# Sums over the features of a linear-attention branch: from VectorE reductions to identity products on TensorE

## The chip, the core and the metric

The kernel runs on one core of a Trainium2 chip. The metric is device time in microseconds (us) for one execution of the whole program. Five engines work side by side, each with its own instruction queue: PE (TensorE, matrix products; PEld is its loading of weights), ACT (ScalarE), DVE (VectorE), POOL (GpSimd) and SP (SyncE, which here issues DMAs). They are tied together by semaphores only. Matrix products read SBUF and write PSUM; ACT and DVE carry results out of PSUM.

## The reference

The inputs are x (1 x 2048 x 512), two sets of projections, and a gate vector. The result is `g * a + (1 - g) * b` with `g = sigmoid(sum(x * gate_w))`. Both branches have 32 heads of 16 features.

- Branch B is plain softmax attention over 2048 keys, followed by an output projection.
- Branch A is linear attention. For queries and for keys it forms `p = q @ w_phi` (16 values per head) and takes `phi = concat(softmax(p), softmax(-p))`, 32 features per head. Then `kv = phi_k^T v`, `z = sum(phi_k)`, and the output is `(phi_q kv) / (phi_q z + 1e-6)`, again followed by an output projection.

The change concerns the denominators of those two softmaxes of branch A: for each token and each head the sum of 16 exponentials of `p` and of 16 exponentials of `-p`, so 64 sums per token, for keys and for queries.

## The kernel before

Branch B fills most of the time. The scores are made transposed, 128 keys by 512 queries at a time: 4 chunks of queries, 32 heads and 16 key tiles give 2048 such tiles, one matrix product each (`qk_mm`, L1283). They are cut into 32 blocks of 64 tiles. In each block a fixed number of tiles (the list `DN`, 712 in all) is exponentiated by DVE and POOL with integer arithmetic (`add_group`, L1360 or L1350 for two tiles at once, then `shifted`, L1336, on POOL), and the other 1336 go in pairs to ACT, 668 instructions of 128x1024 (`add_exp`, L1374). For ACT two pairs of PSUM banks are used in turn, so PE writes a pair of scores while ACT works on the other. The products with V accumulate in one more bank, psO (`pv_mm`, L1395). The last three PSUM banks (`MISC`) are shared by all else: the scores for DVE, every projection, and everything of branch A.

Branch A is spread through the run, one tile of 128 tokens (`st`) at a time. `phi(1, st)` projects the keys (four products, L1044), ACT takes both exponentials out of PSUM (two instructions, L1651), and DVE sums 16 neighbours for each head and sign (`tensor_reduce`, 128x1024 to 128x64, L1657). After each second tile DVE takes the reciprocals of both tiles' sums (L1671). The values of the same tokens are projected (`va_fill`) and written to SBUF twice, once multiplied by the reciprocal for each sign (L1633, two DVE instructions), and POOL copies the reciprocals beside them (L1637). `kv_half` then multiplies `phiK` with these scaled values over eight token tiles. `phi(0, st)` does the same for queries, but there only the ratio of the two sums is formed (reciprocal L1664, product L1666) and the second half of the features is multiplied by it (`scaled_q`, L1683); the tile goes to DRAM, comes back transposed by DMA (`q_turn`), and meets `kv` in `z_rest` (L1740, L1746) and `q_rest` (L1753, L1759). With 16 token tiles for keys and 16 for queries there are 32 sums on L1657, in 16 pairs.

`fill` adds a group of products on PE that takes a bank of `MISC`, cut into operations of `chunk` products; `drain` adds the instruction that reads the bank and, with `last`, frees it. `Plan.layout` orders all operations on the five queues by priorities and estimated durations. Where PE would have nothing to do it puts in an idle operation, four products with zero weights (`zero_mm`, L1385). `Plan.settle(MOVES)` then changes that order by hand-kept lists: for each engine pairs (from, to) of places in its queue, two-tile merges on DVE, banks, and under "drop" the places on PE of idle operations that are left out. So the order on each queue is fixed when the program is built. Before the change PE's queue has 2653 operations, 111 of them idle ones; "drop" names 173 places, and the highest place on PE to which an operation is moved is 2652, the last one.

Features in `phiK`, `EA` and the weights `Wp` lie in the order head group (8), sign (2), head in the group (4), feature (16), the feature innermost. `mask64` and `mask4` cut the products of unlike heads from `kv`.

Of the kernel before, what the change touches and what calls it, by code (L numbers as in the profile page):

```python
# [11 lines left out]
ALU = mybir.AluOpType  # L12
AX = mybir.AxisListType

S = 2048
D = 512
# [49 lines left out]
VA_LAG = 2  # L66
# [25 lines left out]
    ),  # L92
    "act": (
# [3 lines left out]
    ),  # L97
# [786 lines left out]
def _build(ctx, nc, A_x, A_wqkv, A_w_phi, A_wo, B_wqkv, B_wo, gate_w, out):  # L884
# [20 lines left out]
    Ty = sb([128, 2, 2048], name="Ty")  # L905
    vaug = sb([128, NT, VAW], name="vaug")
    vAf = sb([128, 8 * 8 * 2 * 68], name="vA")
    vA = vAf[:].rearrange("p (a b s c) -> p a b s c", a=8, b=8, s=2)
    phiK = sb([128, 8, 1024], name="phiK")
    Ebuf = sb([128, EPAIRS, 512 * (SZ[0] + SZ[1])], name="E")  # L910

# [728 lines left out]
    def phi(qk, st, prio):  # L1640
# [18 lines left out]
        if b == 0:  # L1659
            return  # L1660
# [257 lines left out]
```

## Time and profile before

| what | value |
|---|---|
| median of 3 runs | 680.75 us (680.67 to 681.05) |
| the profiled execution | 680.21 us, its span 678.2 us |
| PE busy | 669.4 us (99%) |
| ACT busy | 654.9 us (97%) |
| DVE busy | 618.0 us (91%) |
| POOL busy | 383.4 us (57%) |
| ACT on the 668 exponentials of branch B (L1374) | 624.7 us |
| DVE on the 32 sums (L1657) | 38.7 us |
| granted TensorE clock | 1.000 |

The span runs from the first to the last instruction. A group of instructions is named by its line, engine and operation, then what it writes and reads ("psS<-qz_t,kTB_t" is a product of two tiles into PSUM). After the bar stand the busy time of the group and the mean of one in nanoseconds. PE's rows overlap: a matrix product's row lasts until its modelled end, while the next one starts earlier, so the distance between starts tells PE's pace and the length of a row doesn't. A busy PE includes the idle operations.

### The profile page before, as it was taken

To read this page: it belongs to the slowest core of one execution; us is meant where nothing else is said; L and a number is where in the kernel's file an instruction comes from. 1 tells how busy PE (TensorE), PEld (TensorE's weight loads), DVE (VectorE), ACT (ScalarE), POOL (GpSimd) and SP (SyncE) were. 2 spreads that over 40 slices of the span, in tenths; PEclk is the share of its full clock that TensorE was granted. 3 is DMA by queue.
4 is the path that set the end of the run, shared out by engine and by line. 5 is a ranking of instruction groups with operands and counts; after the bars stand their busy time and mean duration, and the time that the engine had idled before them with its cause. 6 is when DMAs were issued, how large, how long until landed. Compare 5 with 4: busy or idle time off the path is not lost.

```text
span 678.2 us, 20089 instructions
## 1 busy us (share of the span) xinstructions
PE 669.4 (99%) x8563; PEld 217.5 (32%) x8563; DVE 618.0 (91%) x959; ACT 654.9 (97%) x739; POOL 383.4 (57%) x419
## 2 busy tenths in 40 slices
PE   8999999999999999999999999999999999999997
PEld 4333333333332333323322223322333233333333
DVE  4699899899999999988999989999899999999983
ACT  6999999999999999999998999999999999999995
POOL 7066367453656545455477665676464755565843
PEclk9999999999999999999999999999999999999999
DMA  6810101001010000100113022121321224123221
GB/s 132 159 32 11 31 14 27 11 10 23 7 27 11 10 20 10 28 7 15 22 37 89 26 68 73 46 51 47 69 85 26 70 74 105 34 65 75 65 71 41
DMA packets 67465, 30.90 MB, mean 46 GB/s; under 512 B 52697, under 2 KB 62297, under 8 KB 67377
## 3 DMA queue, kind: packets, MB, share of 16 engines
q1 hardware_dynamic: 66368, 28.95, 17.8%
q8 instruction: 67, 1.10, 0.7%
q10 hardware_dynamic: 576, 0.52, 0.2%
q0 software_dynamic: 432, 0.15, 0.2%
q14 instruction: 22, 0.17, 0.1%
HBM read 7.87 MB, written 8.88 MB: 25 GB/s over the span
## 4 chain that ended last, share of the span: by engine, by line
PE 78%; ACT 14%; DVE 5%; DMA 1%; issue 0%; SPq 0%; DVEq 0%
PE psS L1283 28%; PE psO L1395 27%; PE psS L1044 14%; ACT E_t L1374 13%; PE psO L1385 3%; DVE Tx_t L1360 2%; PE psS L1148 1%; PE psS L1135 1%; PE psS L1696 1%; DMA Lq_t<-ld 1%; DVE Ty_t L1360 1%; ACT EA_t L1651 1%; DMA ld<-Tf_t 1%; PE psS L1753 1%; PE psS L996 0%
## 5 line engine op out<-in xcount | busy, mean ns | idle before, releaser
L1374 ACT ACTIVATE E_t<-psS 128x1024 bf16<-128x1024 f32 x668 | 624.7, 1061 | 11.9 <-PE psS L1283 11.4
L1283 PE MATMUL psS<-qz_t,kTB_t 32*128 32x512 bf16 x2048 | 285.3, 384 | 3.1 <-ACT E_t L1374 1.1
L1360 DVE TENSOR_SCALAR Tx_t<-psS 128x512 int16<-128x512 f32 x232 | 154.5, 684 | 10.4 <-PE psS L1283 8.9
L1283 PEld LDWEIGHTS psS<-qz_t,kTB_t 32*128 32x128 bf16 x2048 | 74.0, 91 | 245.4 <-ACT E_t L1374 108.9
L1395 PE MATMUL psO<-E_t,vaug_t 128*32 128x512 bf16 (+1 forms) x1336 | 109.7, 384 | 0.0
L1336 POOL INT64_ADD vA_t<-vA_t x69 | 67.8, 988 | 25.7 <-PE psO L1395 21.6
L1360 DVE TENSOR_SCALAR Ty_t<-psS 128x512 int16<-128x512 f32 x106 | 71.0, 681 | 4.3 <-PE psS L1283 3.3
L1336 POOL INT64_ADD Ty_t<-Tx_t x28 | 28.2, 1007 | 51.5 <-DVE Tx_t L1360 41.6
L1336 POOL INT64_ADD Ty_t<-Ty_t x39 | 39.6, 1016 | 19.5 <-PE psO L1395 18.4
L1395 PE MATMUL psO<-vA_t,vaug_t 128*32 128x512 bf16 (+1 forms) x494 | 47.3, 382 | 0.0
L1360 DVE TENSOR_SCALAR oT_t<-psS 128x512 int16<-128x512 f32 x60 | 40.1, 683 | 4.1 <-PE psS L1283 3.5
L1395 PE MATMUL psO<-Ty_t,vaug_t 128*32 128x512 bf16 (+1 forms) x414 | 42.0, 384 | 0.0
L1044 PE MATMUL psS<-Wp_t,xT_t 128*32 128x512 bf16 x512 | 40.4, 382 | 0.1
L1360 DVE TENSOR_SCALAR Tz_t<-psS 128x512 int16<-128x512 f32 x58 | 38.1, 684 | 2.4 <-PE psS L1283 2.1
L1044 PE MATMUL psS<-xT_t,WB_t 128*32 128x512 bf16 x464 | 40.0, 383 | 0.0
L1385 PE MATMUL psO<-xT_t,zero_t 128*32 128x512 bf16 x408 | 38.8, 385 | 0.5 <-DVE Tf_t L1489 0.4
L1395 PEld LDWEIGHTS psO<-E_t,vaug_t 128*32 128x32 bf16 x1336 | 26.4, 95 | 39.6 <-issue 30.4
L1360 DVE TENSOR_SCALAR vA_t<-psS 128x512 int16<-128x512 f32 x52 | 34.9, 683 | 1.3 <-PE psS L1283 1.1
L1360 DVE TENSOR_SCALAR WAT_t<-psS 128x512 int16<-128x512 f32 x50 | 33.4, 682 | 2.2 <-PE psS L1283 1.9
L1360 DVE TENSOR_SCALAR Wp_t<-psS 128x512 int16<-128x512 f32 x46 | 30.8, 679 | 0.4 <-PE psS L1283 0.3
L1336 POOL INT64_ADD WoB_t<-oT_t x17 | 17.2, 1013 | 19.4 <-DVE oT_t L1360 15.8
L1395 PE MATMUL psO<-Tx_t,vaug_t 128*32 128x512 bf16 x268 | 27.8, 387 | 0.0
(162 smaller groups left out, 904.5 us busy)
## 6 DMA issues: line engine op xcount, KB each, us to landing
dpq<-EA_t SPq DMA_DIRECT2D x16, 256.0 KB, 2.3
Rb_t<-lr SPq DMA_DIRECT2D x120, 32.0 KB, 1.8
dpo<-kv_t SPq DMA_DIRECT2D x16, 128.0 KB, 1.7
qz_t<-qz_t SPq DMA_DIRECT2D x120, 16.0 KB, 1.8
Tf_t<-Tf_t SPq DMA_DIRECT2D x60, 32.0 KB, 2.0
WB_t<-in_B_wqkv_dram SPq DMA_DIRECT2D x3, 384.0 KB, 4.3
out_dram<-WvA_t SPq DMA_DIRECT2D x8, 128.0 KB, 2.0
out_dram<-WB_t SPq DMA_DIRECT2D x6, 128.0 KB, 1.9
```

The lines of the kernel that those rows point to most:

```text
L1044: ins = e.matmul(out[32 * i:32 * i + 32, :], lhsT=lhsT[:, 32 * i:32 * i + 32], rhs=rhs, start=start, stop=stop, tile_position=(0, 32 * i))
L1135: mms = [lambda e, ap, i=i, t=t: e.matmul(ap[:, 128 * i:128 * (i + 1)], lhsT=xT[:, t, NQ * c + 128 * i:NQ * c + 128 * (i + 1)], rhs=W_B[:, ...
L1148: mms = [lambda e, ap, i=i, t=t: e.matmul(ap[:, 256 * i:256 * (i + 1)], lhsT=xT[:, t, NQ * c + 128 * (2 * hf + i):NQ * c + 128 * (2 * hf + ...
L1283: return e.matmul(bank, lhsT=kT_B[32 * i:32 * i + 32, ROW[b // 2] % 2, 128 * kt:128 * (kt + 1)], rhs=qz[32 * i:32 * i + 32, b // 2 % 4, b ...
L1336: op = P.add("pool", P64 + W64 * size, d_prio(g["ts"][0]) - 5.0 + (0.0 if key == "s" else M_LATE), lambda e: e.int64_add(words(dst), words ...
L1360: ops.append(drain(f, mm, "dve", 0.70, d_prio(d), lambda e, ap, q=q: e.tensor_scalar(quarter(tb, q).bitcast(I16), ap, EXPB, 0.0, op0=ALU.a ...
L1374: op = P.add("act", EXP_OVH + 0.4267 * n, 0.0, lambda e: e.activation(Ebuf[:, j // 2 % EPAIRS, 512 * SZ[0] * (j % 2):512 * SZ[0] * (j % 2) ...
L1385: ins = e.matmul((psO if bank is None else bank)[32 * i:32 * i + 32, :], lhsT=zero[:], rhs=xT[:, 0, 0:NQ], start=bank is not None, stop=ba ...
L1395: return e.matmul(psO[32 * i:32 * i + w, :], lhsT=vaug[:, kt, o:o + w], rhs=rhs, start=start, stop=stop, tile_position=(0, 32 * i), skip_g ...
L1651: ins = e.activation(dst.rearrange("p (g s c) -> p s g c", s=2, c=64)[:, sgn, :, :], ap.rearrange("p (g c) -> p g c", c=64), ACTF.Exp, sca ...
L1696: ins = e.matmul(ap[64 * s:64 * s + 64, 68 * gg:68 * gg + 68], lhsT=phiK[:, m, 128 * g + 64 * s:128 * g + 64 * s + 64], rhs=vA[:, m, g, s, ...
L1753: mms = [lambda e, ap, g=g: e.matmul(ap[:, 64 * g:64 * g + 64], lhsT=qT(g)[:, 128 * j:128 * (j + 1)], rhs=kzbd[:, g, 0:64], start=True, st ...
```

## The change

The sums over 16 features leave DVE. For each pair of token tiles PE now multiplies an identity matrix with the exponentials, once for each of the 16 features, and accumulates: 32 products of 128x128 weights with 64 columns, in four operations of eight, into 128 columns of one `MISC` bank (`fill` named S). DVE takes the reciprocals directly out of that bank (keys: one instruction for both tiles; queries: the reciprocal of the second half, and a copy of the first half to `statq` for the later denominator). The projection of the values now waits for these products (`after = [mm]`) and not for a DVE operation.

So that one product reads four neighbouring elements at a time, the features are laid out with the four heads of a group innermost: head group, sign, feature, head. That is done where `Wp` is copied from PSUM (a permuted output), and `scaled_q`, the masks and the views of `stat` and `statq` follow. `mask4` is made by a DVE sum of the identity and one POOL copy in place of a POOL fill and four POOL copies. The two multiplications of V become one DVE instruction with 128x1024 outputs, and `vA` has the sign ahead of the head group.

All lists of `MOVES` are other ones. "drop" names 207 places (173 before), the highest place on PE is 2696 (2652 before). `DN`, the slots of ACT and all other constants stay. Of `MOVES` only ACT's list is shown; its first numbers are places in the queue as laid out, its second ones the places to which operations are moved.

```diff
@@ -63,7 +63,7 @@
-VA_LAG = 2
+S_PRIO = -2.0
@@ -80,341 +80,350 @@
 MOVES = {
...
     "act": (
-        (87, 80), (105, 85), (127, 104), (133, 122), (131, 124), (136, 128), (149, 145), (151, 148), (158, 167), (179, 220), (181, 222), (185, 241),
-        (197, 244), (211, 249), (215, 257), (238, 263), (244, 279), (268, 287), (277, 356), (304, 375), (331, 378), (379, 412), (383, 419), (413,
-        456), (415, 459), (442, 505), (444, 509), (484, 525), (486, 553), (516, 584), (520, 589), (564, 619), (568, 630),
+        (87, 79), (105, 82), (127, 101), (132, 114), (137, 123), (139, 126), (155, 141), (157, 146), (177, 166), (198, 218), (200, 221), (201, 241),
+        (218, 244), (238, 251), (242, 256), (244, 266), (249, 281), (268, 288), (277, 357), (330, 376), (332, 379), (350, 412), (359, 419), (390,
+        454), (394, 458), (408, 504), (417, 509), (427, 524), (446, 552), (480, 584), (488, 589), (530, 618), (543, 630),
...
@@ -905,7 +914,7 @@
     vAf = sb([128, 8 * 8 * 2 * 68], name="vA")
-    vA = vAf[:].rearrange("p (a b s c) -> p a b s c", a=8, b=8, s=2)
+    vA = vAf[:].rearrange("p (a s b c) -> p a s b c", a=8, b=8, s=2)
@@ -1030,10 +1039,8 @@
     wbd_ops = [dma("pool", -4, lambda e, j=j: e.dma_start(Wbd[16 * j:16 * j + 16, :, 16 * j:16 * j + 16], wphi_v[j]),
                    [("Wbd", j)], reads=["Wbd0"], name=f"wbd{j}", issue=0.8, lat=3.0) for j in range(8)]
     P.join_writes(wbd_ops, "Wbd")
-    pool(0.1, -2, lambda e: e.memset(mask4[:], 0.0), writes=["mask40"], name="mk0")
-    P.join_writes([P.add("pool", 0.15, -2, lambda e, q=q: e.tensor_copy(mask4[32 * q:32 * q + 32, 2 * (q % 2):2 * (q % 2) + 2],
-                                                                      half2[32 * q:32 * q + 32, :]), reads=["half2", "mask40"],
-                         name=f"mk1{q}") for q in range(4)], "mask4")
+    small(lambda e: e.tensor_reduce(quad[:, 0:4], ident[:].rearrange("p (k j) -> p j k", j=4), AX.X, ALU.add), ["ident"], ["quad"], "mk0", -2)
+    pool(0.15, -2, lambda e: e.tensor_copy(mask4[:], quad[:, 0:4]), reads=["quad"], writes=["mask4"], name="mk1")
     pool(0.2, -2, lambda e: e.tensor_copy(mask64[:].rearrange("p (j c) -> p j c", c=16), mask4[:].unsqueeze(2).to_broadcast([128, 4, 16])),
          reads=["mask4"], writes=["mask64"], name="mk2")
@@ -1618,7 +1625,8 @@
                                            rhs=Wbd[:, r, :], start=True, stop=True) for r in range(KT)]
         f, mm = fill(prio, mms, ["Wbd"] + [("WAT", 4 * qk + r) for r in range(KT)], name=f"W{qk}{t}", chunk=4,
                      dur=0.07, cols=128)
-        wp_ops.append(drain(f, mm, "dve", 0.69, prio, lambda e, ap: e.tensor_copy(Wp[:, t, D * qk:D * (qk + 1)], ap),
+        wp_ops.append(drain(f, mm, "dve", 0.69, prio, lambda e, ap: e.tensor_copy(
+            Wp[:, t, D * qk:D * (qk + 1)].rearrange("p (a f j) -> p a j f", j=4, f=DH), ap.rearrange("p (a j f) -> p a j f", j=4, f=DH)),
                             writes=[("Wp", qk, t)], name=f"We{qk}{t}"))
     va_ops = []
@@ -1628,13 +1636,13 @@
         f, mm = fill(prio, proj([xT[:, t, 128 * st:128 * (st + 1)] for t in range(KT)],
                                 [WvA[:, t, :] for t in range(KT)]), ["WvA"] + xk(st // 4), name=f"VA{st}", after=after, kind="col")
         va_ops.append(mm)
-        by = stat[:, b, :].rearrange("p (g s j) -> p g s j", s=2, j=4)
-        for s in range(2):
-            drain(f, mm, "dve", 0.70, prio, lambda e, ap, s=s: e.tensor_tensor(
-                vA[:, m, :, s, 0:64].rearrange("p g (j d) -> p g j d", j=4), ap.rearrange("p (g j d) -> p g j d", g=8, j=4),
-                by[:, :, s, :].unsqueeze(3).to_broadcast([128, 8, 4, DH]), ALU.mult),
-                reads=[("rs", b), ("ss", b)], writes=[("vA", m, s)], name=f"VAe{st}.{s}", last=s == 1)
-        P.add("pool", 0.3, prio, lambda e: e.tensor_copy(vA[:, m, :, :, 64:68], by), reads=[("rs", b), ("ss", b)],
+        by = stat[:, b, :].rearrange("p (s g j) -> p s g j", s=2, j=4)
+        drain(f, mm, "dve", 1.24, prio, lambda e, ap: e.tensor_tensor(
+            vA[:, m, :, :, 0:64].rearrange("p s g (j d) -> p s g j d", j=4),
+            ap.rearrange("p (g j d) -> p g j d", g=8, j=4).unsqueeze(1).to_broadcast([128, 2, 8, 4, DH]),
+            by.unsqueeze(4).to_broadcast([128, 2, 8, 4, DH]), ALU.mult),
+            reads=[("rs", b)], writes=[("vA", m, s) for s in range(2)], name=f"VAe{st}")
+        P.add("pool", 0.3, prio, lambda e: e.tensor_copy(vA[:, m, :, :, 64:68], by), reads=[("rs", b)],
               writes=[("vA", m, 2)], name=f"VAr{st}")
     def phi(qk, st, prio):
@@ -1652,25 +1660,27 @@
                                    ap.rearrange("p (g c) -> p g c", c=64), ACTF.Exp, scale=1.0 - 2.0 * sgn)
             return ins
         drain(f, mm, "act", 0.98, -4, both, writes=[dkey], name=f"ex{qk}.{st}")
-        e3 = dst.rearrange("p (g f) -> p g f", f=DH)
-        sums, skey = (stat[:, b, :], ("ss", b)) if qk else (statq[:, st % 8, :], ("sq", st % 8))
-        P.add("dve", 1.22, prio, lambda e: e.tensor_reduce(sums, e3, AX.X, ALU.add), reads=[dkey], writes=[skey],
-              name=f"ss{qk}.{st}")
         if b == 0:
             return
+        es = [(phiK[:, i % 8, :], ("phiK", i % 8)) if qk else (EA[:, i % 2, :], ("EA", i % 2)) for i in (st - 1, st)]
+        mms = [lambda e, ap, n=n, f=f: e.matmul(ap[:, 64 * n:64 * n + 64].rearrange("p (s g j) -> p s g j", s=2, j=4), lhsT=ident[:],
+                                                rhs=es[n][0].rearrange("p (g s f j) -> p f s g j", s=2, f=DH, j=4)[:, f],
+                                                start=(f == 0), stop=(f == DH - 1)) for n in range(2) for f in range(DH)]
+        f, mm = fill(S_PRIO + prio, mms, [k for _, k in es] + ["ident"], name=f"S{qk}.{st}", chunk=8, dur=0.042, cols=64)
         if qk == 0:
-            both_q = statq[:, st % 8 - 1:st % 8 + 1, :].rearrange("p b (g s j) -> p (b g) s j", s=2, j=4)
-            r3 = ratio[:].rearrange("p b (g j) -> p (b g) j", j=4)
-            P.add("dve", 0.4, prio, lambda e: e.reciprocal(r3, both_q[:, :, 1, :]), reads=[("sq", st % 8 - 1), ("sq", st % 8)],
-                  writes=["ratio"], name=f"rs{qk}.{st}")
-            P.add("dve", 0.25, prio, lambda e: e.tensor_tensor(r3, r3, both_q[:, :, 0, :], ALU.mult),
+            three = lambda ap: ap[:, 0:128].rearrange("p (b s c) -> p b s c", b=2, s=2)
+            drain(f, mm, "dve", 0.55, prio, lambda e, ap: e.reciprocal(ratio[:], three(ap)[:, :, 1, :]), writes=["ratio"],
+                  name=f"rs{qk}.{st}", last=False)
+            drain(f, mm, "dve", 0.25, prio, lambda e, ap: e.tensor_copy(statq[:, st % 8 - 1:st % 8 + 1, 0:32], three(ap)[:, :, 0, :]),
+                  writes=[("sq", st % 8 - 1), ("sq", st % 8)], name=f"rp{qk}.{st}")
+            P.add("dve", 0.25, prio, lambda e: e.tensor_tensor(ratio[:], ratio[:], statq[:, st % 8 - 1:st % 8 + 1, 0:32], ALU.mult),
                   reads=["ratio", ("sq", st % 8 - 1), ("sq", st % 8)], writes=["ratio"], name=f"rt{qk}.{st}").lock = True
             for i in (st - 1, st):
                 scaled_q(i, prio)
             return
-        P.add("dve", 0.62, prio, lambda e: e.reciprocal(stat[:], stat[:]), reads=[("ss", 0), ("ss", 1)],
+        drain(f, mm, "dve", 0.96, prio, lambda e, ap: e.reciprocal(stat[:], ap[:, 0:128].rearrange("p (b c) -> p b c", b=2)),
               writes=[("rs", 0), ("rs", 1)], name=f"rs{qk}.{st}")
-        after = [P.ops[-VA_LAG]]
+        after = [mm]
         for i in (st - 1, st):
             va_fill(i, prio, after)
@@ -1678,8 +1688,8 @@
     def scaled_q(st, prio):
         b = st % 2
-        minus = EA[:, b, :].rearrange("p (g s j f) -> p g s j f", s=2, j=4, f=DH)[:, :, 1, :, :]
-        by = ratio[:, b, :].rearrange("p (g j) -> p g j", j=4).unsqueeze(3).to_broadcast([128, 8, 4, DH])
+        minus = EA[:, b, :].rearrange("p (g s f j) -> p g s f j", s=2, j=4, f=DH)[:, :, 1, :, :]
+        by = ratio[:, b, :].rearrange("p (g j) -> p g j", j=4).unsqueeze(2).to_broadcast([128, 8, DH, 4])
         P.add("dve", 0.7, prio, lambda e: e.tensor_tensor(minus, minus, by, ALU.mult),
               reads=["ratio", ("EA", b)], writes=[("EA", b)], name=f"phi0.{st}.1").lock = True
         q_write(st)
@@ -1694,7 +1704,7 @@
                     def one(e, ap, g=g, gg=gg, m=m):
                         for s in range(2):
                             ins = e.matmul(ap[64 * s:64 * s + 64, 68 * gg:68 * gg + 68], lhsT=phiK[:, m, 128 * g + 64 * s:128 * g + 64 * s + 64],
-                                           rhs=vA[:, m, g, s, :], start=(m == 0), stop=(m == 7), tile_position=(0, 64 * s))
+                                           rhs=vA[:, m, s, g, :], start=(m == 0), stop=(m == 7), tile_position=(0, 64 * s))
                         return ins
                     mms.append(one)
             f, mm = fill(prio, mms, [("phiK", m) for m in range(8)] + [("vA", m, s) for m in range(8) for s in range(3)],
@@ -1742,9 +1752,9 @@
         f, mm = fill(prio, mms, [("phiQT", g) for g in range(8)] + ["kz1"], name=f"Z{n}", chunk=8, dur=0.028, cols=60, after=n_ops[-1:])
         n_ops.append(mm)
         dr = denr[:, n % 2, :]
-        plus = statq[:, 4 * (n % 2):4 * (n % 2) + 4, :].rearrange("p b (g s j) -> p (b g) s j", s=2, j=4)[:, :, 0, :]
+        plus = statq[:, 4 * (n % 2):4 * (n % 2) + 4, 0:32]
         drain(f, mm, "dve", 0.25, -3, lambda e, ap: e.scalar_tensor_tensor(
-            dr.rearrange("p (h j) -> p h j", j=4), plus, 1e-6, ap[:, 0:128].rearrange("p (h j) -> p h j", j=4), ALU.mult, ALU.add),
+            dr.rearrange("p (b c) -> p b c", b=4), plus, 1e-6, ap[:, 0:128].rearrange("p (b c) -> p b c", b=4), ALU.mult, ALU.add),
               reads=[("sq", 4 * (n % 2) + j) for j in range(4)], writes=[("dr", n % 2)], name=f"na{n}")
         P.add("dve", 0.9, -3, lambda e: e.reciprocal(dr, dr), reads=[("dr", n % 2)], writes=[("dr", n % 2)], name=f"nb{n}")
```

641 rows, old and new, of the table MOVES are left out of this document.

## The prediction

> **What bounds the kernel now.** I read the page's busy times and its chain of work first, then ACT's waits, then a table of windows that I cut where PE's idle operations become rare or frequent.
>
> ```profile
> PE 669.4 (99%) x8563; PEld 217.5 (32%) x8563; DVE 618.0 (91%) x959; ACT 654.9 (97%) x739; POOL 383.4 (57%) x419
> PE 78%; ACT 14%; DVE 5%; DMA 1%; issue 0%; SPq 0%; DVEq 0%
> ```
> ```profile
> ACT E_t L1374 <- PE psS L1283: 11.4, 29, 1.4
> ```
>
> PE and ACT are nearly full. ACT's work stays as it is, so all that a better order can win is the time in which ACT waits for scores: 11.4 us in 29 waits. PE carries 78% of the chain, DVE 5%. The change takes work from DVE and gives some to PE, so the question is where PE has room. Its room shows as idle operations (L1385, four rows each). First all engines by window (window, length, then PE, PEld, DVE, ACT, POOL busy), then the rows of L1385 alone:
>
> ```profile
> 71.00:132.00 61.00, 60.97 (x821) 21.68 (x817) 56.64 (x89) 59.52 (x71) 33.62 (x37) 1.00 0.09 22
> 132.00:192.00 60.00, 59.91 (x798) 19.07 (x798) 56.20 (x88) 59.97 (x69) 32.26 (x37) 1.00 0.07 14
> 192.00:283.00 91.00, 90.81 (x1167) 29.02 (x1155) 87.75 (x134) 89.74 (x106) 49.61 (x58) 1.00 0.07 15
> 283.00:340.00 57.00, 56.84 (x759) 18.84 (x756) 52.12 (x76) 56.99 (x64) 28.95 (x30) 1.00 0.09 18
> 340.00:382.00 42.00, 41.27 (x500) 12.22 (x496) 41.37 (x69) 38.05 (x43) 29.96 (x31) 1.00 0.17 53
> 382.00:680.00 298.00, 291.02 (x3775) 91.50 (x3771) 270.35 (x413) 285.63 (x321) 174.51 (x177) 1.00 0.24 62
> ```
> ```profile
> 71.00:132.00 61.00, 1.59 (x16) 0.42 (x16) 1.00 0.09 22
> 132.00:192.00 60.00, 4.76 (x48) 1.36 (x52) 1.00 0.07 14
> 192.00:283.00 91.00, 0.79 (x12) 0.12 (x8) 1.00 0.07 15
> 283.00:340.00 57.00, 4.74 (x48) 1.23 (x48) 1.00 0.09 18
> 340.00:382.00 42.00, 2.57 (x24) 0.63 (x24) 1.00 0.17 53
> 382.00:680.00 298.00, 19.95 (x216) 5.02 (x216) 1.00 0.24 62
> ```
>
> The reader is to see three kinds of stretch. From 132 to 192 and from 283 to 340 us ACT is full (0.03 and 0.01 us idle) and PE has 12 idle operations in each: ACT is the bound and PE has room. From 71 to 132 and from 192 to 283 us PE has 4 and 3 idle operations in 152 us, and ACT is idle for 1.48 and 1.26 us: PE is the bound. From 340 to 382 us DVE is busy for 41.37 of 42 us and ACT is idle for 3.95 us: DVE is the bound.
>
> **The sums leave DVE.**
>
> ```profile
> L1657 DVE TENSOR_REDUCE statq_t<-EA_t 128x64 f32<-128x1024 bf16 x16 | 19.4, 1210 | 0.4 <-ACT EA_t L1651 0.4
> L1657 DVE TENSOR_REDUCE stat_t<-phiK_t 128x64 f32<-128x1024 bf16 x16 | 19.3, 1207 | 0.5 <-ACT phiK_t L1651 0.4
> L1633 DVE TENSOR_TENSOR vA_t<-psS,stat_t 128x512 bf16<-128x512 f32 x32 | 20.7, 681 | 0.1
> L1671 DVE RECIPROCAL stat_t<-stat_t 128x128 f32<-128x128 f32 x8 | 7.5, 944 | 0.0
> L1664 DVE RECIPROCAL ratio_t<-statq_t 128x64 f32<-128x64 f32 x8 | 4.4, 545 | 0.0
> L1666 DVE TENSOR_TENSOR ratio_t<-ratio_t,statq_t 128x64 f32<-128x64 f32 x8 | 1.7, 214 | 0.0
> L1621 DVE CAST Wp_t<-psS 128x512 bf16<-128x512 f32 x8 | 5.4, 686 | 0.4 <-PE psS L1617 0.2
> L1350 DVE TENSOR_SCALAR Tx_t<-psS 128x1024 int16<-128x1024 f32 x18 | 22.0, 1221 | 1.6 <-PE psS L1283 1.4
> ```
>
> Gone are 19.4 + 19.3 = 38.7 us. Scaling V in one instruction has no row; the nearest is a 128x1024 read of PSUM, L1350, 1.22 us, so 16 x 1.22 = 19.5 us take the place of 20.7 (bounds: 1.22 and the 1.36 of two old ones). The reciprocals now read PSUM; I keep their 0.94 and 0.55. New are 8 copies of 128x64, priced as L1666, 8 x 0.21 = 1.7 us. DVE: 618.0 - 38.7 - 1.2 + 1.7 = about 580 us, 85% of the span. The masks (one DVE sum of 128 columns at the start, POOL with four instructions fewer), the permuted copy of Wp (8 times) and `scaled_q` with its other broadcast change forms, not counts; none is on the path, since DVE keeps about 98 us free, and I take zero. If the permuted write ran at half speed, it would cost 8 x 0.69 us on an engine that has them. No DMA is added or taken away; SP's order is another one, and its queue is no part of the chain.
>
> Relief of DVE moves the end only where DVE is the bound. How much of it lies there is told by the windows of L1657:
>
> ```profile
> 71.00:132.00 61.00, 4.83 (x4) 1.00 0.09 22
> 192.00:283.00 91.00, 9.68 (x8) 1.00 0.07 15
> 340.00:382.00 42.00, 2.42 (x2) 1.00 0.17 53
> ```
>
> From 340 to 382 us two sums go, 2.42 us, and one copy of 0.21 comes: a credit of 2.2 us, between nothing (another DVE operation is late there next) and ACT's whole idle time of 3.95 us. The place of the longest wait, in the timeline, shows how such a sum acts: it delays the reading of a bank, PE's next scores wait for the bank, and ACT for PE.
>
> ```profile
> 368.83 1.21 DVE L1657 TENSOR_REDUCE statq_t<-EA_t 128x64 f32<-128x1024 bf16 x1
> 371.30 0.39 PE L1283 MATMUL psS<-qz_t,kTB_t 32*128 32x512 bf16 x2 [0.31 <-DVE Wp_t L1360]
> 372.96 1.94 ACT L1374 ACTIVATE E_t<-psS 128x1024 bf16<-128x1024 f32 x2 [1.41 <-PE psS L1283]
> ```
>
> **The sums come to PE.** Each of 16 pairs adds 32 products of 64 columns with full 128x128 weights. The same shape is L1753. Timeline rows of one run of eight, then of an idle operation, then two long runs from the chain:
>
> ```profile
> 510.74 0.60 PE L1283 MATMUL psS<-qz_t,kTB_t 32*128 32x512 bf16 x3
> 511.28 0.29 PE L1753 MATMUL psS<-kzbd_t,phiQT_t 128*128 128x64 bf16 x4
> 511.41 0.28 PE L1753 MATMUL psS<-kzbd_t,WAT_t 128*128 128x64 bf16 x4
> 511.62 0.39 PE L1283 MATMUL psS<-qz_t,kTB_t 32*128 32x512 bf16 x3
> ```
> ```profile
> 302.51 0.39 PE L1395 MATMUL psO<-WoB_t,vaug_t 128*32 128x512 bf16 x4
> 302.73 0.39 PE L1385 MATMUL psO<-xT_t,zero_t 128*32 128x512 bf16 x4
> 303.05 0.39 PE L1283 MATMUL psS<-qz_t,kTB_t 32*128 32x512 bf16 x3
> ```
> ```profile
> 159.64 1.00 PE psS L1135 x16
> 499.61 0.89 PE psS L1740 x32
> ```
>
> Four products take 511.41 - 511.28 = 0.13 us, 0.033 us each; the eight and the step to the scores take 0.34, so leaving costs 0.08. The idle operation's step to the scores is 0.32 where its like takes 0.22 (302.51 to 302.73): a change of tiling costs 0.10. A pair in one run is 32 x 0.033 = 1.05 us, with entering and leaving 1.23. Most slots of ACT are entered and left once on PE anyway, so I take 1.15 us. The low end is the pace of L1740 (4 columns), 0.89 us; the high end that of L1135 (128 columns), 32 x 1.00 / 16 = 2.0 us. I stay near L1753 because the shape is the same; what differs is that the moving operand comes in runs of four elements, for which this trace has no row.
>
> [...]
>
> All of PE: 16 x 1.15 = 18.4 us come. The lists say what goes: PE's last place moves from 2652 to 2696, 44 more operations, and 16 x 4 = 64 are new, so the 111 idle ones become 91. 20 x 0.22 = 4.4 us go, 14.0 us net stay; that is the bill if PE were the bound everywhere.
>
> By window: ACT's list puts the branch's exponentials in nearly the old places (80 to 630 before, 79 to 630 after), so the pairs stay where they are. The windows of L1657 put two pairs between 71 and 132 us and four between 192 and 283, where PE has no room: 6 x 1.15 = 6.9 us, less the seven idle operations there, 7 x 0.22 = 1.5, is 5.4 us. The other ten pairs (11.5 us) stand beside 84 idle operations (18.5 us) and cost nothing while these last.
>
> ```profile
> L1374 ACT ACTIVATE E_t<-psS 128x1024 bf16<-128x1024 f32 x668 | 624.7, 1061 | 11.9 <-PE psS L1283 11.4
> ```
>
> New waits: S stands in PE's queue until ACT has both exponentials of the second tile done, and the next scores are queued behind it. The order hides that, if S stands a slot later; without this cover ACT loses up to one exponential, 1.06 us, per pair. S also holds one of the three shared banks until DVE's reciprocal, some 1.15 + 0.94 us, 16 times, 2% of what three banks have in 678 us; zero on the path, at most one 0.68 us read of scores late per pair. V's projection waits for S and no longer for a sum; its scaling waits for the reciprocal as before.
>
> **Sum.** Profiled time 680.21 + 5.4 - 2.2 = 683.4 us. The profiled execution lies 0.54 us under the median, so 684.0 us. With the ends of both terms, 6 x 0.89 - 1.5 - 3.95 and 6 x 2.0 - 1.5, this case spans 680.6 to 691.3.
>
> **Rivals.**
> Faster: the two stretches without room borrow from their neighbours. The 24 idle operations from 132 to 192 and from 283 to 340 us lie right beside them, and score tiles for DVE or products with V can be early or late by more than that. Then the 5.4 us vanish and DVE's relief counts: all of 3.95 us in the DVE-bound stretch and a little of the rest, some 4 us in all, 676.8 us. Against it: those idle operations stood there before, and PE was full next door all the same. It decides once less than 2.2 of the 5.4 us stay.
> No change: debit and credit cancel, near 680.75, because ACT fills most of the run.
> Much slower: S is dearer than L1753. At 2.0 us a pair, torn into four runs of eight, each entered and left for 0.18, a pair is 2.7 us, and 6 x 2.7 - 1.5 = 14.7 us: 695. At 2.0 us in one run, with the credit, 6 x 2.0 - 1.5 - 2.2 = 8.3: 689. The bill of PE everywhere, 14.0 us, ends at the same place. For it speaks the missing row for short runs, against it that PE shows no pace over 0.0625 us for so few columns.
> [...]
>
> **How the numbers follow.** A difference under 0.2% (1.4 us) can't be told from none here. Forecast 0.45, faster rival 0.27, no change 0.11, much slower 0.17. So faster 0.27, same 0.11, slower 0.62. The range reaches into the faster rival and up to the middle of the much slower one, 676.5 to 693; the forecast's own is 681 to 691.
>
> **What would show it.** Right: no TENSOR_REDUCE of 1024 elements; 364 rows of idle operations; the products of S starting 0.030 to 0.035 us apart; DVE near 580 us; ACT idle by some 4 to 7 us between 71 and 283 us instead of 2.7, and by about 2 instead of 3.95 between 340 and 382. Wrong: ACT stays full from 71 to 283 us (faster rival), starts over 0.05 us apart (much slower), or a score product waiting for an exponential of branch A behind S (the hidden wait).

## The result, and the profile after

The changed kernel takes 682.81 us (median of 8 runs, 682.26 to 683.59) against 680.76 us for the kernel before (8 runs, 680.13 to 681.2). The ratio is 1.0032, 95% interval 1.0021 to 1.0042: slower, by more than the 0.2% that a measurement can tell. The forecast was 684.0 us. The time came out where the sum put it, but two of its three terms were wrong, and it takes the profile to see that.

The profiled execution of after took 682.9 us, its span is 680.7 us. First its busy times, the engine shares of its chain and ACT's longest wait:

```profile
PE 670.5 (99%) x8995; PEld 232.9 (34%) x8995; DVE 591.1 (87%) x920; ACT 656.2 (96%) x739; POOL 383.2 (56%) x415
PE 78%; ACT 15%; DVE 5%; DMA 1%; issue 0%
```
```profile
ACT E_t L1381 <- PE psS L1290: 11.6, 34, 1.1
```

DVE lost 26.9 us of work (618.0 to 591.1), PE has 432 products more, ACT waits about as long as before (11.6 against 11.4 us). By these totals nearly nothing happened. The groups of DVE and PE that answer to the terms of the sum (lines have moved by 7 to 10):

```profile
L1640 DVE TENSOR_TENSOR vA_t<-psS,stat_t 128x1024 bf16<-128x1024 f32 x16 | 19.5, 1217 | 0.9 <-PE psS L1051 0.7
L1628 DVE CAST Wp_t<-psS 128x512 bf16<-128x512 f32 x8 | 10.2, 1298 | 0.0
L1681 DVE RECIPROCAL stat_t<-psS 128x128 f32<-128x128 f32 x8 | 7.6, 951 | 0.3 <-PE psS L1666 0.3
L1674 DVE COPY statq_t<-psS 128x64 f32<-128x64 f32 x8 | 1.4, 173 | 0.0
L1392 PE MATMUL psO<-xT_t,zero_t 128*32 128x512 bf16 x328 | 32.0, 385 | 0.0
L1392 PE MATMUL psS<-xT_t,zero_t 128*32 128x512 bf16 x36 | 3.2, 386 | 0.1
```

V's scaling, the reciprocals, the copy and the 364 rows of idle operations are as priced. One row isn't: the permuted copy of `Wp` takes 1298 ns where the plain one took 686.

Where the time went shows best when the k-th of the 668 exponentials of branch B (L1374 before, L1381 after) is compared with the k-th of the other trace. The exponentials are counted from 0. The table has the start of one before, and by how much it starts later in other kernels (us, from the traces; "write only" is experiment 2 and "read permuted" the second run of experiment 1, both told below):

| exponential | start before | after | write only | read permuted |
|---|---|---|---|---|
| 20 | 27.1 | -0.21 | +0.07 | -0.71 |
| 60 | 64.2 | +3.56 | +2.90 | -0.86 |
| 180 | 184.5 | +4.36 | +3.04 | -0.04 |
| 360 | 366.9 | +4.51 | +3.00 | -0.16 |
| 380 | 388.1 | +2.95 | +2.99 | -1.71 |
| 560 | 563.8 | +3.13 | +3.12 | -1.53 |
| 667 | 669.5 | +2.49 | +3.09 | -2.32 |

In the column "after" 3.8 us arise between 27 and 64 us, where the prediction looked for nothing. The two stretches without room for the sums, from 71 to 283 us, add less than 1 us, and 1.6 us come back between 367 and 388 us. The windows say the same. Here ACT alone (window, length, ACT busy, clock, share and rate of DMA), first before, then after:

```profile
27.00:64.00 37.00, 36.99 (x41) 1.00 0.18 42
71.00:283.00 212.00, 209.23 (x243) 1.00 0.08 17
340.00:389.00 49.00, 44.79 (x50) 1.00 0.16 47
```
```profile
27.00:64.00 37.00, 34.06 (x37) 1.00 0.16 38
71.00:283.00 212.00, 208.66 (x242) 1.00 0.07 17
340.00:389.00 49.00, 46.32 (x53) 1.00 0.16 48
```

From 27 to 64 us ACT was full before and is idle for 2.94 us after. From 71 to 283 us its idle time goes from 2.77 to 3.34 us. From 340 to 389 us it falls from 4.21 to 2.68.

What stands between 27 and 64 us is the set of eight permuted copies. Timeline rows of after (start, length, engine, line; idle time ahead and its releaser in brackets):

```profile
39.75 2.42 DVE L1628 CAST Wp_t<-psS 128x512 bf16<-128x512 f32 x2
42.22 0.38 PE L1290 MATMUL psS<-qz_t,kTB_t 32*128 32x512 bf16 x1 [0.72 <-DVE Wp_t L1628]
43.51 1.94 ACT L1381 ACTIVATE E_t<-psS 128x1024 bf16<-128x1024 f32 x2 [0.87 <-PE psS L1290]
```

Two copies hold DVE for 2.42 us. PE's scores for DVE wait for the bank that the second copy frees, and ACT's scores are queued behind them: ACT stops for 0.87 us.

### The profile page after: what moved, and what is told of

Read it like the earlier page. It is cut to its first block, busy times and chain, and to the rows that moved or that the text cites. A ratio compares the mean times of both kernels' runs of the same rounds, so it can differ in the third digit from the quotient of the medians.

```text
span 680.7 us, 20896 instructions
## 1 busy us (share of the span) xinstructions
PE 670.5 (99%) x8995; PEld 232.9 (34%) x8995; DVE 591.1 (87%) x920; ACT 656.2 (96%) x739; POOL 383.2 (56%) x415
## 4 chain that ended last, share of the span: by engine, by line
PE 78%; ACT 15%; DVE 5%; DMA 1%; issue 0%
PE psO L1402 28%; PE psS L1290 27%; PE psS L1051 15%; ACT E_t L1381 14%; PE psO L1392 2%; PE psS L1666 2%; DVE Wp_t L1628 1%; PE psS L1763 1%; DMA ld<-Tf_t 1%; PE psS L1142 1%; PE psS L1155 1%; PE psS L1750 1%; DVE Tz_t L1367 1%; DVE Ty_t L1357 1%; PE psS L1005 0%; DVE Tx_t L1367 0%
## 5 line engine op out<-in xcount | busy, mean ns | idle before, releaser
L1381 ACT ACTIVATE E_t<-psS 128x1024 bf16<-128x1024 f32 x668 | 625.2, 1054 | 12.9 <-PE psS L1290 11.6
L1290 PE MATMUL psS<-qz_t,kTB_t 32*128 32x512 bf16 x2048 | 275.4, 384 | 4.2 <-DVE Wp_t L1628 1.5
L1290 PEld LDWEIGHTS psS<-qz_t,kTB_t 32*128 32x128 bf16 x2048 | 71.9, 91 | 236.3 <-ACT E_t L1381 114.6
L1402 PE MATMUL psO<-vA_t,vaug_t 128*32 128x512 bf16 x494 | 48.0, 383 | 0.0
L1343 POOL INT64_ADD phiQT_t<-Tx_t x18 | 17.9, 992 | 41.0 <-DVE Tx_t L1367 34.6
L1402 PEld LDWEIGHTS psO<-E_t,vaug_t 128*32 128x32 bf16 (+1 forms) x1336 | 27.3, 95 | 38.2 <-issue 27.1
L1051 PE MATMUL psS<-xT_t,WB_t 128*32 128x512 bf16 x464 | 38.0, 383 | 0.1
L1051 PE MATMUL psS<-Wp_t,xT_t 128*32 128x512 bf16 x512 | 37.8, 382 | 0.0
L1343 POOL INT64_ADD vA_t<-Tx_t x20 | 19.9, 998 | 25.8 <-DVE Tx_t L1367 24.6
L1392 PE MATMUL psO<-xT_t,zero_t 128*32 128x512 bf16 x328 | 32.0, 385 | 0.0
```

Of the source, the lines that this page charges most:

```text
L1051: ins = e.matmul(out[32 * i:32 * i + 32, :], lhsT=lhsT[:, 32 * i:32 * i + 32], rhs=rhs, start=start, stop=stop, tile_position=(0, 32 * i))
L1290: return e.matmul(bank, lhsT=kT_B[32 * i:32 * i + 32, ROW[b // 2] % 2, 128 * kt:128 * (kt + 1)], rhs=qz[32 * i:32 * i + 32, b // 2 % 4, b ...
L1343: op = P.add("pool", P64 + W64 * size, d_prio(g["ts"][0]) - 5.0 + (0.0 if key == "s" else M_LATE), lambda e: e.int64_add(words(dst), words ...
L1381: op = P.add("act", EXP_OVH + 0.4267 * n, 0.0, lambda e: e.activation(Ebuf[:, j // 2 % EPAIRS, 512 * SZ[0] * (j % 2):512 * SZ[0] * (j % 2) ...
L1392: ins = e.matmul((psO if bank is None else bank)[32 * i:32 * i + 32, :], lhsT=zero[:], rhs=xT[:, 0, 0:NQ], start=bank is not None, stop=ba ...
L1402: return e.matmul(psO[32 * i:32 * i + w, :], lhsT=vaug[:, kt, o:o + w], rhs=rhs, start=start, stop=stop, tile_position=(0, 32 * i), skip_g ...
```

## The experiments

**1. The copy alone: read permuted, write in one run.** The same elements go to the same places, but the permutation is put on the side of PSUM.

```diff
-    Wp[...].rearrange("p (a f j) -> p a j f", j=4, f=DH), ap.rearrange("p (a j f) -> p a j f", j=4, f=DH)
+    Wp[...].rearrange("p (a f j) -> p a f j", j=4, f=DH), ap.rearrange("p (a j f) -> p a f j", j=4, f=DH)
```

> The changed kernel with one edit: the copy of Wp out of PSUM reads its source permuted and writes its target in one run (before it read in one run and wrote permuted). Theory copy: the 2.1 us of slowdown are the eight copies that went from 686 to 1298 ns; with a row back near 0.69 us ACT's idle time between 27 and 64 us falls from about 3 us to under 0.6, and the time to 679.6 to 680.6. Theory room on PE (the step of the prediction): the slowdown is the sums on PE from 71 to 283 us, DVE has free time for longer copies, so the time stays at 682.8 within 0.7. Should the row stay near 1.3 us, the run tells nothing between the two.

Measured: 678.89 us (11 runs, 677.89 to 680.54), before on the same chip 680.40, ratio 0.9972 (0.9948 to 0.9995). The same kernel on another chip, run again for the later experiments:

> The kernel with the permuted read of Wp once more, beside the next three on the same chip: 678.9 within 0.6, with some executions near 680 whose mean granted clock is 0.997 and others near 678.3 at 1.000.

It took 679.12 us (12 runs), before 680.55, ratio 0.9974 (0.9953 to 0.9996). The first time lies below the range that was expected of it. The group of the copy and ACT's window from 27 to 64 us in the first of the two:

```profile
L1628 DVE CAST Wp_t<-psS 128x512 bf16<-128x512 f32 x8 | 5.4, 684 | 0.0
```
```profile
27.00:64.00 37.00, 36.99 (x42) 1.00 0.18 41
```

The copy is back at 684 ns, ACT is full again, and 3.9 us are gone (682.81 to 678.89; 3.6 us when each is set against the kernel before on its own chip). So the order of the accesses in eight instructions decides whether the whole change loses or wins. This version is 1.5 and 1.4 us faster than the kernel before on the two chips, which is just above the 0.2% that a measurement can tell.

**2. The copy alone, in the kernel before.** Only the permuted write is put into the kernel before; its features then lie in the wrong order, so its output is another one, at the same work.

```diff
-    e.tensor_copy(Wp[:, t, D * qk:D * (qk + 1)], ap)
+    e.tensor_copy(Wp[...].rearrange("p (a f j) -> p a j f", j=4, f=DH), ap.rearrange("p (a j f) -> p a j f", j=4, f=DH))
```

> The kernel before with one edit, the changed kernel's permuted write of Wp; the rest keeps the old order of features, so its sums run over mixed heads. Theory copy: 8 copies of 1.30 us, the start of the exponentials falls behind by 1.5 to 3.3 us between 27 and 64 us, time 682.3 to 684.1. Theory room on PE: 680.8 within 0.7.

Measured: 683.59 us (10 runs, 683.12 to 684.5) against 680.40, ratio 1.0041 (1.0016 to 1.0065). Its group, and ACT's window:

```profile
L1621 DVE CAST Wp_t<-psS 128x512 bf16<-128x512 f32 x8 | 10.2, 1321 | 0.2 <-PE psS L1617 0.2
```
```profile
27.00:64.00 37.00, 35.09 (x39) 1.00 0.15 36
```

One edit makes the kernel before as slow as the changed one, and the column "write only" of the table shows the loss arise at the same place and stay constant from there. Why DVE could not hide it is told by its own rows for this window, first before, then here:

```profile
27.00:64.00 37.00, 35.18 (x53) 1.00 0.18 42
```
```profile
27.00:64.00 37.00, 35.91 (x49) 1.00 0.15 36
```

DVE had 1.8 us free there, and eight copies bring 8 x 0.635 = 5.1. The difference, 3.3 us, is an estimate (DVE isn't quite full here either), and about the 3.1 us by which the last exponentials are late.

**3. The sums on PE, cut to an eighth.** Only 2 of the 16 features are summed, with 4 products where 32 stood; the operations and their order stay.

```diff
-    ... stop=(f == DH - 1)) for n in range(2) for f in range(DH)]
+    ... stop=(f == 1)) for n in range(2) for f in range(2)]
-    ..., name=f"S{qk}.{st}", chunk=8, dur=0.042, cols=64)
+    ..., name=f"S{qk}.{st}", chunk=1, dur=8 * 0.042, cols=8 * 64)
```

> The changed kernel with the same order and the same four operations for each pair, but only 2 of 16 features are summed: 4 products where there were 32, so PE has some 13 us less to do. Leaves out most of the sums. Theory room on PE: the debit of 5.4 us goes, time 677.5 to 679. Theory copy: the sums were covered by room that the order found elsewhere, time 681.3 to 682.8, and the delay between 27 and 64 us stays.

Measured: 682.60 us (10 runs, 682.01 to 683.56), ratio 1.0024 (1.0000 to 1.0048). About 13 us of PE's work are gone (448 products at 0.0295) and the time is 0.2 us shorter than after's. PE's waits for ACT, here and in the kernel of experiment 1 (its second run):

```profile
PE psS L1290 <- ACT E_t L1381: 5.2, 16, 0.5
```
```profile
PE psS L1290 <- ACT E_t L1381: 0.7, 2, 0.5
```

With the short sums PE waits 16 times for ACT, 14 of them within 1.2 us of the products of S; the other two waits stand in the trace of after as well. So in the new order the sums aren't what holds ACT up, and the debit of 5.4 us isn't there. The delay from 27 to 64 us stays whole: the 60th exponential is 3.07 us late.

**4. The sums on PE, doubled.** On the kernel of experiment 1 each product of S is issued twice, the second time into another 128 columns.

```diff
-    mms = [lambda e, ap, n=n, f=f: e.matmul(ap[:, 64 * n:64 * n + 64]..., lhsT=ident[:], rhs=..., ...) ...]
+    def twice(e, ap, n, f):
+        for k in (2, 0):
+            ins = e.matmul(ap[:, 64 * (n + k):64 * (n + k) + 64]..., lhsT=ident[:], rhs=rhs, ...)
+        return ins
+    mms = [lambda e, ap, n=n, f=f: twice(e, ap, n, f) ...]
```

> As the first run, with every sum product issued twice (the second one into unused columns): 512 more products, at 0.030 us some 15 us more on PE. Theory covered (PE waits for ACT's banks about as long as the sums take): 679 to 683. Theory edge (the sums fit just so, PE has no further room): most of it shows, 688 to 694.

Measured: 692.42 us (4 runs, 692.22 to 692.57), ratio 1.0163 (1.0118 to 1.0208): 13.3 us more than experiment 1's second run. ACT from 71 to 283 us, first in that run, then here, and PE's rows of S here (L1669; window, length, PE, PEld):

```profile
71.00:283.00 212.00, 208.87 (x243) 1.00 0.07 17
```
```profile
71.00:283.00 212.00, 202.99 (x235) 1.00 0.07 16
```
```profile
71.00:132.00 61.00, 4.31 (x128) 3.96 (x128) 1.00 0.08 21
132.00:192.00 60.00, 4.47 (x128) 4.05 (x128) 1.00 0.05 12
192.00:283.00 91.00, 8.78 (x256) 8.05 (x256) 1.00 0.06 15
283.00:340.00 57.00, 0.00 (x0) 0.00 (x0) 1.00 0.08 20
```

From 71 to 283 us ACT loses 5.9 us of busy time. By the starts of the exponentials the run falls 7.4 us behind between the 60th and the 283rd; busy time shows less of it, since rows of ACT overlap where it runs without a stop (in the trace of after seven exponentials take 6.65 us from 35.99 us on, while the mean row is 1.054). Eight pairs stand there (64 rows each), so 8 x 32 x 0.0295 = 7.6 us of products were added: every added product costs its full time. That holds from 132 to 192 us too, beside nine idle operations: two pairs, 1.9 us, were added there, and between the 120th and the 180th exponential 1.8 us are lost. Over the whole run the last exponential falls 14.1 us behind, for 15.1 us of added products. Most of the difference is one pair in the DVE-bound stretch: between the 340th and the 380th exponential, where it stands, only 0.3 us are lost. Taking the sums away gains next to nothing, adding as much again costs nearly all of it: in this order they fit just so.

**5. Without the four heads side by side.** The kernel after with the features innermost as before, so that a product reads single elements 32 bytes apart; the masks, `scaled_q` and the plain copy of `Wp` follow.

```diff
-    rhs=es[n][0].rearrange("p (g s f j) -> p f s g j", s=2, f=DH, j=4)[:, f]
+    rhs=es[n][0].rearrange("p (g s j f) -> p f s g j", s=2, f=DH, j=4)[:, f]
```

> The changed kernel with features innermost as before: Wp is copied in one run, and each sum product reads single elements 32 bytes apart where it read four neighbours. If a moving operand in runs of 2 bytes streams like one in a row, the products stay 0.030 us apart, the copies are 0.69 us, and the time is that of the run with the permuted read (theory copy: 679.6 to 680.6; theory room on PE: 682.8 within 0.7). If each element costs more, say 0.06 to 0.12 us a product, PE gets 15 to 45 us more and the time is 690 to 720 by either theory.

Measured: 746.34 us (6 runs, 743.45 to 750.2), ratio 1.0959 (1.0906 to 1.1012). Timeline rows of PE around one run of 16 products, here, and in experiment 1's second run:

```profile
226.80 1.97 PE L1665 MATMUL psS<-phiK_t,ident_t 128*128 128x64 bf16 x16
228.71 0.39 PE L1290 MATMUL psS<-qz_t,kTB_t 32*128 32x512 bf16 x2
```
```profile
211.23 0.64 PE L1666 MATMUL psS<-phiK_t,ident_t 128*128 128x64 bf16 x16
211.80 0.39 PE L1290 MATMUL psS<-qz_t,kTB_t 32*128 32x512 bf16 x2
```

From the first product to the next scores it takes 1.91 us with single elements and 0.57 with runs of four. Less 0.10 for leaving, that is 0.113 and 0.029 us a product. For 512 products the difference is 43 us; the time is 67 us above that of experiment 1, whose copy is as fast, and above the range that was expected. The rest isn't taken apart: the granted clock fell too, to a mean of 0.954 over the 743.9 us of the profiled execution. If it was 0.50 wherever it fell, as in experiment 8, that is 68 us at half clock (an estimate from the mean), enough to hold the rest.

**6. Runs of two.** The kernel of experiment 1, where a product reads runs of two elements, 64 bytes apart.

```diff
-    mms = [... ap[:, 64 * n:64 * n + 64].rearrange("p (s g j) -> p s g j", s=2, j=4), ...
-           rhs=es[n][0].rearrange("p (g s f j) -> p f s g j", s=2, f=DH, j=4)[:, f], ...
+    mms = [... ap[:, 64 * n:64 * n + 64].rearrange("p (s g j) -> p s g j", s=4, j=2), ...
+           rhs=es[n][0].rearrange("p (s g f j) -> p f s g j", s=4, f=DH, j=2)[:, f], ...
```

> As the kernel with the permuted read, but each sum product reads its 64 elements in runs of two (4 bytes) 64 bytes apart where it read runs of four; it sums other elements than it should. With runs of four the products start 0.029 us apart, with single elements 0.113. If two elements in a run are enough, the products stay 0.029 to 0.035 us apart and the time is 678 to 681. If the cost goes by the number of runs (64 runs cost 0.113), 32 runs cost some 0.06 us, PE gets 14 us more and the time is 689 to 694.

One run: 691.08 us. The one run of the kernel before beside it took 689.26 us at a mean granted clock of 0.984, so this run is compared by its trace, which has a clock of 1.000: the span is 688.8 us against 675.8 in experiment 1's second run, 13.0 more. A pair in one run, and the next scores:

```profile
345.54 1.98 PE L1666 MATMUL psS<-EA_t,ident_t 128*128 128x64 bf16 x32
347.45 0.39 PE L1290 MATMUL psS<-qz_t,kTB_t 32*128 32x512 bf16 x3
```

32 products take 1.91 us, less 0.10, or 0.057 each; 512 x 0.028 = 14.3 us more than with runs of four. That bears out experiment 4: a dearer product costs nearly its whole surplus.

**7. DVE's sums put back beside the products.** On the kernel of experiment 1 two sums of 128x512 elements, with unused results, stand ahead of each scaling of V and each `scaled_q`.

```diff
+    def again(e):
+        for _ in range(2):
+            e.tensor_reduce(spare[...], xT[:, 0, 0:512].rearrange("p (g f) -> p g f", f=128), AX.X, ALU.add)
-    lambda e, ap: e.tensor_tensor(
+    lambda e, ap: again(e) or e.tensor_tensor(
-    lambda e: e.tensor_tensor(minus, minus, by, ALU.mult)
+    lambda e: again(e) or e.tensor_tensor(minus, minus, by, ALU.mult)
```

> As the run above, with DVE's work put back: ahead of each scaling of V and each scaling of the queries' second half DVE sums 512 elements twice into a tile that nobody reads, 32 times about 1.2 us. Theory relief (DVE's free time is what the order lives on: it won 1.5 us between 340 and 389 us and lets scores for DVE ride beside those for ACT): ACT's idle time grows in the stretches where DVE was full, time 681.5 to 690. Theory order (the new order alone is better, DVE has time in plenty): 678.9 to 680.

Measured: 723.57 us (6 runs, 721.5 to 730.9), ratio 1.0653 (1.0594 to 1.0712). DVE's total and the sums:

```profile
PE 686.9 (96%) x8995; PEld 234.7 (33%) x8995; DVE 624.2 (87%) x984; ACT 661.4 (92%) x739; POOL 383.4 (53%) x415
```
```profile
L1695 DVE TENSOR_REDUCE spare_t<-xT_t 128x4 f32<-128x512 bf16 x64 | 40.7, 677 | 0.9 <-PE psS L1052 0.7
```

With nearly the same DVE work as before the change (624.2 against 618.0 us) the kernel now takes 44 us more, far above the range that was expected. A part of it is the clock: its mean was 0.967 to 0.983 in the six executions, and the profiled one, at 0.983 over 719.3 us, lost as much as 24 us at 0.50 would take (an estimate from the mean). The new order needs the freed time of DVE; but the sums here stand in front of instructions that free a bank, a worse place than they had before, so 44 us isn't what the change saved. The run shows the direction and no size.

**8. One idle operation ahead of the thin products.** Experiment 1's kernel has executions of two kinds: in 9 of 23 the mean granted clock was 0.997, and those took 679.81 to 680.84 us, the others at most 679.36. Its first profile is of that kind, with one stretch at half clock; of the other eight only the mean is on record, which fits one such stretch (half of 3.40 us is 0.0025 of the 678.2 us). Two windows (PE, PEld, DVE, ACT, POOL, then the clock) and timeline rows:

```profile
413.10:416.50 3.40, 3.40 (x61) 1.64 (x57) 3.37 (x6) 3.40 (x5) 0.00 (x0) 1.00 0.00 0
416.50:419.90 3.40, 3.40 (x28) 0.61 (x27) 2.55 (x5) 2.37 (x3) 1.49 (x2) 0.50 0.47 171
```
```profile
415.90 0.24 PE L1750 MATMUL psS<-kzbd_t,WAT_t 128*128 128x4 bf16 x4
416.07 0.39 PE L1290 MATMUL psS<-qz_t,kTB_t 32*128 32x512 bf16 x2
416.39 1.43 PE L1402 MATMUL psO<-E_t,vaug_t 128*32 128x512 bf16 x10
```

Behind a block of products of 4 columns (L1750, from 414.78 us) the clock is 0.50 for 3.40 us, from 416.50 to 419.90. The edit puts four products with zero weights, 512 columns each, ahead of the first such block, to see whether the stretch stays away:

```diff
+    if n == 0:
+        mms[0] = lambda e, ap, plain=mms[0]: zero_mm(e, ap) and plain(e, ap)
```

> As the first run, with one idle operation (four products with zero weights, 0.2 us, and a change of tiling) ahead of the first group of 128 products of four columns (z_rest of chunk 0, near 414.8 us). Theory clock (in some executions the granted clock is halved for one stretch of 3.4 us right behind those thin products, which costs 1.7 us): no execution with a clock of 0.997, median 678.1 to 678.6. Theory noise (the slower executions have another cause): spread and median as in the first run, or 0.3 us more.

Measured: 679.14 us (12 runs, 678.32 to 679.85), ratio 0.9973 (0.9953 to 0.9993). No execution has the clock of 0.997 any more (all twelve have 0.999 or 1.000), but the median is the one of experiment 1 (678.89 and 679.12). The 14 executions of experiment 1 without that stretch have a median of 678.5, so the added operation seems to cost about the 0.7 us that it saves on average.

Why the clock falls there isn't shown: one trace places the half clock behind the thin products, and one edit stands behind that.

## Why the prediction came out near, by wrong steps

**The near time is luck.** The sum left out 3.8 us for the copies and had 4.5 us too much for the stretches without room (5.4 against 0.95). The two errors arise in different stretches, from different causes, and cancel to 0.7 us.

**The permuted copy: wrong.** The prediction said that masks, permuted copy and `scaled_q` "change forms, not counts; none is on the path, since DVE keeps about 98 us free, and I take zero", and priced a slow write at 8 x 0.69 us "on an engine that has them". The price was nearly right (8 x 0.61 = 4.9 us). The cover was not: 98 us is a figure of the whole span, and between 27 and 64 us, where all eight copies stand, DVE had 1.8 us free. The copies cost 3.9 us in the changed kernel (experiment 1) and 3.1 in the kernel before (experiment 2). The windows that the prediction showed began at 71 us, so it never looked at the place.

For elements of 2 bytes 8 bytes apart the permuted write adds (1298 - 684) / 512 = 1.2 ns per column.

**The debit of 5.4 us in the stretches without room: wrong.** ACT was to be idle by 4 to 7 us between 71 and 283 us; it is idle by 3.34 (2.77 before), and experiment 3 shows that the sums hardly hold it up. The step that failed is "where PE has no room". Few idle operations and a busy PE were read as a full PE, with the order of everything else taken as fixed. The new order makes room in a way that idle operations don't show. Counted from the traces, the scores form 787 separate rounds on PE where they formed 824 (a score opens a round when it starts more than 0.06 us behind the one ahead), so more of them start together; between 192 and 283 us it is 99 rounds against 114. PE changes its tiling 1282 times and not 1310. At 0.216 us a round (the distance of two operations of 512 columns) and 0.10 a change that is 8.0 + 2.8 us, with the 20 idle operations 4.4 more: 15.2 us, against 512 x 0.0295 = 15.1 us of new products. This account is worked out, not tested: no run has the new order without the sums' places, and the rounds depend on timing as well (801 in experiment 3, at the same order). Experiment 4 shows PE full from 71 to 283 us now, also from 132 to 192 us, where the prediction read idle operations as room in which sums "cost nothing". An idle operation is an instruction of the fixed queue: the nine there still run when PE is late, and give room only to an order that leaves them out.

**The credit of 2.2 us in the DVE-bound stretch: right in place and about in size.** From 340 to 382 us ACT's idle time falls from 3.95 to 2.10 us ("about 2" was forecast), from 340 to 389 us by 1.5, and the 380th exponential makes up 1.6 us on the 360th. It does so in each column of the table that has the new order, and not where only the write was changed; with sums back on DVE (experiment 7) it makes up only 0.4. These columns have the new order and the freed DVE together, so the share of each isn't shown.

**The price of S: right.** Products start 0.029 us apart (0.030 to 0.035 expected), a bit under L1753's pace (0.033 in the rows that the prediction read). The 364 rows of idle operations, V's scaling at 1.22 us, the reciprocals and the copies hold as well. DVE stands at 591.1 us against some 580. The copies' 4.9 us are part of that. The rest is a matter of counting: rows of DVE overlap a little, and busy time counts an overlap once. Added up row by row DVE's work falls by 33.4 us (678.1 to 644.8), which is the forecast 38.2 less the copies' 4.9; the busy time falls by 26.9.

**The rivals.** The faster one had the debit vanish, as it nearly did, by room that comes from elsewhere. Whether that room was borrowed from the neighbouring stretches, as it said, isn't tested; its time, 676.8, lies 2.1 to 2.3 us below the kernel with the copy mended (678.89 and 679.12). The much slower one, dear products, is what the change would have been without its layout (experiment 5). Against it the prediction held that PE shows no pace over 0.0625 us for so few columns; in the trace of before four transposes of 128 columns (L1768) stand from 4.14 to 4.57 us, 0.107 each. The hidden wait behind S doesn't show: in the traces of after and of experiment 1 PE enters S at 27 places, and at 22 of them S starts 0.31 to 0.32 us behind the operation ahead, which is the pace of 0.216 and one change of tiling; it never starts more than 0.42 behind.

By its true terms the sum is, from the table's column "after": -0.2 up to the 20th exponential, +3.8 where the copies stand, +0.95 from there to 367 us, -1.6 in the DVE-bound stretch, -0.5 behind it. That makes 2.5 us at the last exponential; the two profiled executions differ by 682.9 - 680.21 = 2.7.

## What to carry to other kernels

Cover is local: before an added cost is hidden behind "free time" of an engine, read that engine's busy time in the window where the work stands. An edit that "only changes forms" needs its own price when it changes the step of a read or a write, and the permutation belongs on the side that takes it for nothing (here PSUM's read: 684 ns, where the plain copy took 686 and the permuted write 1298). A full engine in an old order doesn't bound a new order. Cut the new work down and double it to see whether it is on the path, since the two need not agree.

## What the runs showed of the hardware that I had not expected

- A DVE copy of 128x512 from PSUM to bf16 in SBUF takes 684 ns when it reads PSUM in steps of 64 bytes and writes one run, and 1298 to 1321 ns when it writes single 2-byte elements 8 bytes apart.
- PE's pace went with the runs of the moving operand: 29, 57 and 113 ns for 64 columns of bf16 in runs of four, two and one (experiments 1, 6 and 5).
- A block of products of 4 columns was followed by 3.40 us at half clock in one trace; PE's rows fill the whole of the window ahead of it (3.40 of 3.40 us). 9 of 23 executions of that kernel have the mean clock of 0.997 that goes with such a stretch.
